# First loads, mask rows and diagonals of a fused block-sparse attention and gated FFN kernel: other queues, other engines, a new order at the head

## The chip, the cores and the metric

The kernel runs on one core of one Trainium2 chip. The metric is the device time of one execution in microseconds (us). The core has five engines with a queue each: TensorE (PE) for matrix products, VectorE (DVE), ScalarE (ACT), GpSimd (POOL), and SyncE (SP), which here only issues DMAs. ScalarE and GpSimd issue DMAs on their own queues too. Each queue is worked off in order, so an instruction that waits holds everything behind it on its engine.

## The reference

The reference has two parts. The first is block-sparse attention over 4 batches, 8 heads, 768 tokens and a head size of 64, in blocks of 32 tokens:

```
scores = q @ k^T / sqrt(64)
mask   = |blk_i - blk_j| <= 1, or blk_i or blk_j is 0 or 23,
         or blk_j is one of sampled_blocks[blk_i] (3 per query block)
attn   = softmax(where(mask, scores, -1e9));  x = attn @ v
```

The second takes the heads side by side (512 wide) through a gated FFN:

```
h    = relu(x @ w_in)                    # 768 x 1024 per batch
conv = 3-tap convolution of h along the tokens, one weight per channel and tap
out  = (h * sigmoid(conv)) @ w_out       # 768 x 512 per batch
```

## The kernel before

All operations are put in a list, and a string, `ORDER`, says in which order they are issued. Each entry is two characters for the operation's number, then a letter for the engine where the operation has a choice (A ScalarE, V VectorE, G GpSimd), then one character for each buffer that it takes. The priorities and costs beside the operations (`{"DVE": 0.45}`) belong to the planner that wrote the string; when the kernel is built, `put_down` only follows the string. An engine's queue is thus the string's order restricted to that engine. Changing the string changes all queues.

The 16 pairs of heads (four to a batch) go through 144 units of eight 128x128 score blocks. For a unit, TensorE computes scores into one of two `st` buffers (`s`, line 773), ScalarE takes the exponential into `pt` (`exp`, line 785, 128x1024), and TensorE multiplies by v (`av`, line 810). VectorE divides by the row sums (`rcp`, `norm`), and `x_tr` or a DMA transpose turns the result into `xT`. Then come the first weight matrix (`f1`, line 914, with `relu` to `hE`), the three taps (`mul`, line 972, and `add`, line 980, on VectorE), tanh on ScalarE (line 1019), `g1` and `g2` on VectorE (lines 1022 and 1027, into `gT`), and the second weight matrix (`f2`, line 844). For one half of the last batch the three taps run on TensorE instead, as products with diagonal matrices (`conv`, line 991). These matrices, `diag`, are made by `dg` (line 391): 8 channel groups by 3 taps, each an identity matrix of 128x128 times one weight per partition, 24 instructions on VectorE.

The mask is part of the score product. Under the 64 rows of k and q in each slot `t` stand 24 rows (partitions 64 to 87): the k side says to which block a key belongs, the q side holds -8000 for a block that the query may not see. The k side comes from `nblk` (line 283) through `m_k` (two copies, for even and odd k columns). The q side comes from the sampled blocks: `ld_sb` (line 254) loads them into `sbi`, `a4` and `a5` (line 296) make `A` and then `mtok`, in two halves, and `m_q0` copies the first half in the order of the tokens into slot 0 (two copies, of 256 and 128 elements). `m_q1` does so for the second half of the queries. `m_h1` repeats the q rows and the k rows for the second head of the pair, `m_r1` repeats `m_q1`'s. The other slots get their mask rows by copies (`m_sq`, `m_sr`) or DMAs on SyncE's queue (`m_dk`, `m_dq`, `m_sp`); `m_back` holds a reordered copy for the later pairs. Copies made by the helper `dcopy` carry line 324 on ScalarE, 326 on GpSimd and 328 on VectorE.

The first pair's q and k arrive in float32 in the output staging tiles `o2s` (`ld_q0`, `ld_k0`: the first half of the queries of each head, and all keys), and are cast to bf16 into `nat` by `cast_q` and `cast_k`. `k_tr` and `q_tr` turn them on TensorE (lines 474 and 514), and `k_cp` and `q_cp` bring them into slot 0. All later pairs come by GpSimd's queue, already cast. Until the first scores, and in gaps after them, TensorE runs 13 wide and 29 narrow dummy products (`warm`, `fill`, line 230).

In the order before, the first DMAs are: on SyncE the first head's k, the sampled blocks, the second head's q, the convolution weights; on ScalarE the first head's q, then the second head's k. The second head's casts are on GpSimd, between its loads. `m_q0` is on ScalarE, and both `m_h1` on VectorE.

Of the kernel before, what the change touches and what calls it, by code (L numbers as in the profile page):

```python
# [25 lines left out]
6z6i6j6v26A36n6o16D06E2h16F45+06w6I16J6x6B6C6G6R06S6H6K56L6M6W16X6T06Y11v1a2iV6p21r6q2jV6N05/V6O6r16/0706U06V6sV6P0
6QV71274175763in1io7907aiq0ir7i17j7b41p1sipV001d2NV4isViL07k51y4/2+2it17n07oiu6Z6+7p0iMiNiOivV1501z513025231531A54
1B5537056iP7s17t7273iw0ix7x07y2v17u1iyA393103211e330347z277787G17H7c2C02wV2xViT12DV47e12EViU7f7L07M7d17l7I37N4iQiF1
7Q17m7RiG7q7r7V07W7v7wiHV22F07AiR2GV2HV7S57X07B2Q17+17/7J0iz080187088892iA7K8c18d8e32RV0iWiViS0iBV32SV7C27O7P7T8h0
8i7U7Y7Z2T0iX2UV7D8m18j48n818302VViC18v0iDiEV8wiI0821iJiYiZ84iKVi/2j0j738o58x08A18B8a8b8f8g8F08G8C18H28k7g18l8p8q  # L30
8K17E08L8y08P08z7hA18M38518Q8D8E8I8R48r1j2i+7FVj18s86V8X18J8Y8Z58N8O8t0900912/V0j8j38Sja8uV8U235Vj9jl1951jm8T192096
8+8/939a09b94jf0jgj497136Vjbj538V1j69c2jc9i1989j9n0999o9d9ejhjn9k43c19p58Vjd9f0je9s19t9u1573a583b23d113g13hV2593i
3j12I03l3k5a3r3u3v02W13n08W2joji9x09yjjA0jpV19g3eV3fV1o9z39C1jr1jsju0jvjtAjwAjP09l09m9D2J19q9K09Ljx09E0jy9P19Q9M2
9R49r9v9wjQ2KV2LVjzVjSjR9A9U09V9B9FjA19H1jT9W59IjBjCAjX19Z19G19N9+jD0jG1jHa50jEjU9/1jZjVjYjFVj+a6jIAa739Oaa19Sabac0
jM12X09Taf0ag9XjN9Yak1alah4k322YVk42ZVk6j/am5jJ0ap0jKa0aqa1a80a9adax1aeaiajay3x3s23w3G3Dk0k5jLVa22jOVjWk1kb3a3k7k2
kckdkear2anaz1aoaC0aDaskp0aH1aIat1aAaE3aJ0k8aBaM0aFaNaGkB1aU1aKkCaLkqaVaO4aZ0aPaQa+kfkgaW5a/2k9kakrkDb219h9J3o3z13A
3m3a43y4au0khkiksb3kEktA2b433pV3BVkFV3avb70kK0b8kLb90kH13CV3qVbc1aX0kIbdaYkJV14kMAbe53H23E03J3I3S3P3Q13T33Vbk0blkQ0
b0kN1bm1b1kRb5kSAl30aR1l4aSl6l5l7kOkPA5lb1ld3tV3b6bp1bqbr4bakT0bu0bbl83L1jkkukG3M3W0aw03K0aT3UbvkW1kUkVV6bz1bw2bAbf
bg1kXbnbokYAbB3bsbH0kZ0bIbtbxk+bM1bybNl01bJ0k/A7lclj2lklml9bR0bCbSl1kj0bO5bh2lebil2V3FV43NVla1lflr3bW1bXbT1bY4kv1bD
kkb/0bK03RA0bE0llbFlslnc0c71c8c13kwbLbPbQbUkxbVbZb+c90lgcc0cdklkyce53XkzA0bGbjkAjqlulhltlvkmc2c31cach1cbciknV2lo3+  # L40
414213/24643lic41lplwlx3OVlqcj2lF1lz0cm0cnlGlAcu1cvcw1co4lBlHly3YV1lIlJV3cz1lClDV0cAcfcB3cE0lO1cFlPlL03ZVc540V1lQV
cG0lMlNAcgcJ1cKm70cO0cPckcllU1cpcqlVm8m9macr0cL5lR0lSmbcscQ2lWAlTAmf1mccx0cW1cycXcCc/0cDl+1l/d0cHcIcMcNcY4d41d5d13
d65mhmgmdmim0VcRcT2mjlX0lYcS1lZAcZd90c+m11dadh1d2dim40d3m2d7mkdb2dj3dm0dnm5d8dr1ds44454c4f4g04k4h4imemn2momlmqcUm3V
m6VmpkolKc61471lE4l048cVctdo1mJ1dcdw0dxdddk0dldt0dy4mv3mxmrmmmwde1mydfmzdB1dCdpmD0dqdJ0dKdumKdD5msdL3mEdO1dvdzdAdE
dF1dPmtmu4d04t4u2mAdT0dUdMmFdNmLdgdQ1dV0dRdY1mBmCmMdZmGe40dSe5mNV1dG2d+4dWdXm/1e91n04eV249V24aVn1V084j4y4q4r1e65
mHA2eaee0d/e0eb2n50efn21n34mmO4sV3dHe10e24z1dI2eg3ej1ekn6e70eo0epn4Vnn0n7V9np4nV3no4oVel1eq04v4H4I34w4x4E4M4J4F24K
4Lne1e8ew1ecexn80n9ey5edeheieB0nfeCemenereG1eHnaAeD2ngAnb0es1ezeL0nceMeAnh1nv1nqet1eI34S4T0eN1eunrndVanwnD2nxnEny
eT1eEeUnk0eFnieJeKeOePeY0nleV4eZnjAbnseQ2eRnGnz4pe3ev4AeS4N04Oe+0eW0f11nmAf2mP1eXmQe/mRf60f0f7mV0f35f4mSnAf82fb1mW
nFnL3nMnHnBntnOnNmTV3nP4GV44BV4nu0nCnIfcfd1fj0mXfkf5mYfl4fo1f9oc1fpft0odmZA0nQfq0oeVnJo90fafufeoao31obAfg0nK4CVo4
o5Afy1fzo60o7nZ1n+oz0nRfv3fA5o8AoAnSfhoBor1otosoC4PV0ouoDov4QVfG0fHff1n/o0fI2fL1fMoi0fmfnfQ0fRo1A1ojfrof1ogfsfN1fw  # L50
fxfV1fWfS4okAohAoEoH2owfX0nT0ol1fBfCfJ0f+0f/g03fKomfOfPnUg61fTg7g85nVoIoxonVoJoyoFoKgb0gcoo1opfUfD1oLfYfZgg1ghg1nW
# [61 lines left out]
def kernel(  # L113
# [74 lines left out]
    op = gr.op  # L188
# [887 lines left out]
```

## Time and profile before

| | |
|---|---|
| median of 3 runs | 207.18 us (206.76 to 207.27) |
| the profiled execution: its time | 207.02 us |
| its span, first to last instruction | 205.2 us |
| granted TensorE clock | 0.998 |
| TensorE busy | 200.1 us, 98% |
| VectorE busy | 184.7 us, 90% |
| ScalarE busy | 189.4 us, 92% (144 exponentials: 140.3 us) |
| GpSimd busy | 60.0 us, 29% |

A row of the timeline has the start, the duration, the engine, the line of the kernel, the operation, what it writes and reads with the shapes, how many instructions are merged into the row, and in brackets the engine's idle time before it and what ended that. SPq, ACTq and POOL rows named DMA are the issuing of a DMA. A row of the groups has the busy time, the mean duration in ns, and the idle time before. TensorE's products overlap in its pipeline, and their ends are modelled, so a busy TensorE need not be at its full rate.

### The profile page before, as it was taken

The page shows a single profiled execution, that of the slowest core. Times are in us where ns is not written, and L with a number is a line of the kernel's source. Part 1 is how long each engine was busy: PE and PEld are TensorE (multiplying, and loading weights), DVE is VectorE, ACT ScalarE, POOL GpSimd, SP SyncE. Part 2 cuts the span into 40 slices and gives each one's busy share as a digit, 9 for nine tenths or more (in the row PEclk, how much of TensorE's full clock was granted, in tenths as well). Part 3 has the DMA queues.
Part 4 walks back from the last instruction along what each step waited for, and adds up shares of the span by engine and source line. Part 5 has one row for each costly group of instructions (what it writes and reads, how often), then busy time and mean ns, then how long its engine had stood idle before and what let it go on. Part 6 is the DMA issues. An engine that isn't in the chain of part 4 may idle for free.

```text
span 205.2 us, 6315 instructions
## 1 busy us (share of the span) xinstructions
PE 200.1 (98%) x2442; PEld 145.2 (71%) x2442; DVE 184.7 (90%) x577; ACT 189.4 (92%) x252; POOL 60.0 (29%) x116
## 2 busy tenths in 40 slices
PE   7999999999999999999999999999999999999994
PEld 5678877877677766766477667766676767787773
DVE  6999999999999998999899979999999737999970
ACT  5899999999999999999799999999999989998843
POOL 5987634326242423114215334710000000000000
PEclk9999999999999999999999999999999999999999
DMA  6999997999989995999969779994040260001305
GB/s 148 191 179 193 188 201 119 143 120 148 144 110 113 124 143 73 244 123 127 222 106 171 116 103 180 133 136 77 0 139 21 78 227 0 3 0 71 139 29 179
DMA packets 50913, 25.45 MB, mean 124 GB/s; under 512 B 35588, under 2 KB 48740, under 8 KB 50884
## 3 DMA queue, kind: packets, MB, share of 16 engines
q0 software_dynamic: 20000, 11.24, 44.5%
q1 hardware_dynamic: 30452, 13.45, 32.8%
q8 instruction: 19, 0.31, 0.6%
q10 hardware_dynamic: 432, 0.36, 0.6%
q14 instruction: 10, 0.08, 0.1%
HBM read 23.09 MB, written 6.29 MB: 143 GB/s over the span
## 4 chain that ended last, share of the span: by engine, by line
PE 78%; ACT 14%; DVE 4%; issue 3%; ACTq 0%
PE st L773 25%; PE mix L914 18%; PE mix L844 15%; PE av L810 13%; ACT pt L785 10%; PE av L230 2%; DVE t L328 2%; ACT hE L934 2%; ACT m L1019 1%; PE st L844 1%; PE mix L740 1%; PE av L991 1%; ACT o2s L324 1%; DVE diag L391 1%; PE mix L536 1%
## 5 line engine op out<-in xcount | busy, mean ns | idle before, releaser
L785 ACT ACTIVATE pt<-st 128x1024 bf16<-128x1024 f32 x144 | 140.3, 1033 | 4.5 <-PE st L773 3.3
L773 PE MATMUL st<-t 88*128 88x256 bf16 (+2 forms) x600 | 93.0, 268 | 0.5 <-ACT pt L785 0.3
L810 PEld LDWEIGHTS <-pt 128*128 128x128 bf16 x1152 | 55.4, 97 | 13.7 <-ACT pt L785 0.4
L773 PEld LDWEIGHTS <-t 88*128 88x128 bf16 x600 | 48.6, 97 | 20.6 <-issue 1.0
L810 PE MATMUL av<-vt,pt 128*128 128x65 bf16 x1152 | 62.4, 193 | 0.1
L914 PE MATMUL mix<-xT,winb 128*128 128x384 bf16 (+2 forms) x288 | 55.7, 308 | 0.1
L972 DVE TENSOR_SCALAR m<-hE,cw 128x382 bf16<-128x382 bf16 (+2 forms) x192 | 49.9, 318 | 3.8 <-ACT hE L934 3.6
L844 PE MATMUL mix<-woutb,gT 128*128 128x512 bf16 (+2 forms) x200 | 49.6, 360 | 0.0
L980 DVE TENSOR_TENSOR m<-m 128x764 bf16<-128x764 bf16 (+2 forms) x64 | 33.4, 531 | 0.2
L914 PEld LDWEIGHTS <-winb 128*128 128x128 bf16 x288 | 24.1, 97 | 8.6 <-issue 0.7
L1019 ACT ACTIVATE m<-m 128x764 bf16<-128x764 bf16 (+2 forms) x32 | 26.2, 826 | 0.0
L844 PEld LDWEIGHTS <-gT 128*128 128x128 bf16 x224 | 18.7, 97 | 8.8 <-DVE gT L1027 0.3
L419 POOL COPY pace<-pt 1x1 bf16<-1x1 bf16 x24 | 7.6, 317 | 50.3 <-ACT pt L785 50.1
L934 ACT ACTIVATE hE<-mix 128x384 bf16<-128x384 f32 (+2 forms) x39 | 18.9, 504 | 0.9 <-PE mix L914 0.4
L721 DVE TENSOR_TENSOR xtok<-av,rcp 128x384 bf16<-128x384 f32 (+2 forms) x36 | 18.2, 507 | 0.3
L1027 DVE TENSOR_TENSOR gT<-m,hE 128x764 bf16<-128x764 bf16 (+3 forms) x36 | 18.0, 508 | 0.3
L239 POOL DMA_DIRECT2D nat<-in_q_dram x23 | 16.9, 736 | 2.0 <-issue 1.6
L936 DVE TENSOR_SCALAR hE<-mix 128x384 bf16<-128x384 f32 x25 | 13.8, 554 | 1.0 <-PE mix L914 0.7
L328 DVE COPY t<-mix 64x384 bf16<-64x384 bf16 (+1 forms) x34 | 13.8, 410 | 0.8 <-PE mix L536 0.2
L1022 DVE TENSOR_SCALAR m<-m 128x764 bf16<-128x764 bf16 (+3 forms) x36 | 12.1, 342 | 0.6 <-ACT m L1019 0.5
L239 POOL DMA_DIRECT2D vn<-in_v_dram x16 | 11.5, 720 | 1.3 <-issue 0.6
L328 DVE COPY t<-stg 64x1536 bf16<-64x1536 bf16 x20 | 11.6, 586 | 0.3
(74 smaller groups left out, 118.9 us busy)
## 6 DMA issues: line engine op xcount, KB each, us to landing
out_dram<-o2s SPq DMA_DIRECT2D x16, 256.0 KB
vn<-in_v_dram POOLq DMA_DIRECT2D x16, 192.0 KB, 5.1
nat<-in_k_dram POOLq DMA_DIRECT2D x15, 192.0 KB, 5.0
out_dram<-o2s SPq DMA_DIRECT2D x15, 128.0 KB
nat<-in_q_dram POOLq DMA_DIRECT2D x6, 192.0 KB, 4.9
winb<-in_moe_w_in_dram POOLq DMA_DIRECT2D x2, 512.0 KB, 7.6
woutb<-in_moe_w_out_dram POOLq DMA_DIRECT2D x4, 256.0 KB, 7.3
nat<-in_q_dram POOLq DMA_DIRECT2D x9, 96.0 KB, 4.9
```

The costliest lines, as they stand in the source:

```text
L239: return op(name, {eng: occ}, lambda e: on(e).dma_start(out=dst(), in_=src), prio, deps, dma=(kind, service), **kw)
L328: nc.vector.tensor_copy(out=dst, in_=src)
L721: nm = op("norm", {"DVE": t_dps(128 * C)}, lambda e: nc.vector.tensor_tensor(out=xtok_t[xk.index][:, 0:C].rearrange("p c h d -> p h c d"), ...
L773: nc.tensor.matmul(out=st[:, 128 * x:128 * (x + n_)], lhsT=t[0:88, 12 + 6 * hh + kc, :], rhs=t[0:88, idx:idx + (n_ - 1) * (2 if P < NPE el ...
L785: nc.scalar.activation(out=pt_t[ptb.index][:, c0:c1], in_=st_t[stb.index][:, c0:c1], func=AF.Exp, bias=0.0, scale=0.125)
L810: nc.tensor.matmul(out=o[:, off:off + 65], lhsT=pt_t[ptb.index][:, 128 * x:128 * x + 128], rhs=V_t[vslot_b[P].index][:, hh, kc, 0:65], sta ...
L844: nc.tensor.matmul(out=acc(), lhsT=gT_t[gb.index][:, ffc, 128 * t:128 * t + 128], rhs=woutb[:, ffc, c0:c1], start=(ffc == 0), stop=(ffc == ...
L914: nc.tensor.matmul(out=mix_t[hb.index][:, w1 * y:w1 * y + w1], lhsT=winb[:, fc, 128 * ffc:128 * ffc + 128], rhs=xT_t[xt_buf[n].index][:, f ...
L934: nc.scalar.activation(out=dst, in_=src, func=AF.Relu, bias=0.0, scale=0.5)
L972: nc.vector.tensor_scalar(out=m_t[cb.index][:, x, y, 0:w], in0=hE_t[heb.index][:, f0 + y, t0 + x:t0 + x + w], scalar1=cw[:, x, f0 + y:f0 + ...
L980: nc.vector.tensor_tensor(out=m[:, a_, :, 0:w], in0=m[:, a_, :, 0:w], in1=m[:, b_, :, 0:w], op=ALU.add)
L1019: th = [op("tanh", {"ACT": t_act(2 * w) + 0.04}, lambda e, cb=cb, w=w: nc.scalar.activation(out=m_t[cb.index][:, 0, :, 0:w], in_=m_t[cb.in ...
```

## The change

The sampled blocks are loaded first of all on ScalarE's queue, followed by the first head's q; SyncE loads the first head's k, then the second head's k and q. In the new string `m_q0` stands on VectorE, right behind `a5`; the `m_h1` of the q rows stands on ScalarE and that of the k rows on VectorE, later. The second k's cast is on ScalarE. `m_dk` reads the k rows of one head twice, so it no longer waits for `m_h1`. The diagonals are GpSimd's, at the very end of its queue, behind its last load. `he_zero`, `ident24`, `m_r1`, `m_sr` and `m_sp` have other places. From the head up to about a third of the kernel, and in its tail, the string has another order; between these the queues of TensorE, VectorE and ScalarE are as before.

```diff
-0J1f0O0I0K1k0L0002103040M05010P1W01X0N060Q1U0070R080S0+A1CA11EA1FG282090/V1DG0a13V15181b290b1g2610c1h0d1i0e1j0f0U0g
...
+0J1f0O0I0K1k0L0002103040M05010P1W01X0N060Q1U0070R281080S0+A1EA21CA1FA29090/V15181b1DG0a1g2610b1h0c1i0d1j0e0U0f0V0g
...
     k0 = first_k(0, "SP", -22, [])
-    q0 = first_q(0, "ACT", -22, [])
-    k1 = first_k(1, "ACT", -21, [q0])
-    ld_sb = op("ld_sb", {"SP": 0.46}, lambda e: nc.sync.dma_start(
+    ld_sb = op("ld_sb", {"ACT": 0.46}, lambda e: nc.scalar.dma_start(
         out=sbi[64:MR], in_=sampled_blocks.bitcast(I32).rearrange("b r -> (b r)").unsqueeze(0).broadcast_to([NB, 6 * NB])),
-        -21, after=[k0], lat=1.8)
-    q1 = first_q(1, "SP", -20, [ld_sb])
+        -22, lat=1.8)
+    q0 = first_q(0, "ACT", -21, [ld_sb])
+    k1 = first_k(1, "SP", -21, [k0])
+    q1 = first_q(1, "SP", -20, [k1])
...
-            mr = [dma("m_dk", "SP", lambda s=s: T_t[s][64:88, 12:24].rearrange("j c s -> j (c s)"),
-                      T_t[0][64:88, 12:24].rearrange("j c s -> j (c s)"), T(4.5 * s - 4), m_k + m_h1[1:], service=0.4)]
+            mr = [dma("m_dk", "SP", lambda s=s: T_t[s][64:88, 12:24].rearrange("j (h c) s -> j h (c s)", h=2),
+                      T_t[0][64:88, 12:18].rearrange("j c s -> j (c s)").unsqueeze(1).broadcast_to([NB, 2, 768]),
+                      T(4.5 * s - 4), m_k, service=0.4)]
...
-                nc.vector.tensor_scalar(out=diag[:, x, f], in0=ident, scalar1=cw[:, x, f:f + 1], scalar2=None,
+                nc.gpsimd.tensor_scalar(out=diag[:, x, f], in0=ident, scalar1=cw[:, x, f:f + 1], scalar2=None,
                                         op0=ALU.mult)
-        o_diag[f] = op("diag", {"DVE": 3 * t_d4(128)}, dg, T(10 + f), [o_cw, o_ident], earliest=14.0)
+        o_diag[f] = op("diag", {"POOL": 1.2}, dg, T(100 + f), [o_cw, o_ident], earliest=130.0)
```

More of the change, by code (lines that the diff above doesn't have):

```diff
@@ L26 @@
[L26 to L50, printed above, removed]
@@ L61 @@
+ig1qaqyAhhQqIhZqX0qKqYqei31qn1qoi4i74i8qfA2qpAii90hR0ihiiia2ibhSA2qz2qAqBqCij1qDikqt1ic0quidAqh0qvAjqih+1qjh/Ail1qk
+qEimAqlA3rl1rmrnArr0rsqP3qJqFqQqLqSqGqRq+rtAqMqTqNrx1ryru1rvro0rwArprH0rIr31rz2rqArAqOrC1rDr90rBqUpiqgqmpcrJ1rE2qZ
+qVrFq/ras70rM0r4rNsd1rGses8qWr0rKr1rO2rbr5rLsfr2rPrQrcr6rdA0r7A2sgrR0rSs9sarTrUrf1sbV3shArVA1rgrer8sirWscrhrirjArk
+rX0rYrZr+s11r/As0s2s3s4s5Vs6
 """
@@ L440, in kq_transposes @@
                        {"ACT": 0.25, "DVE": 0.28, "POOL": 0.45} if x else {"ACT": 0.25, "DVE": 0.28},
-                       alloc=[] if x else [nb], uses=[nb] if x else []) for x in range(2)]
+                       uses=[nb]) for x in range(2)]
             ck = [cast("cast_k", lambda x=x: nat_t[nb.index][:, 1, 384 * x:384 * x + 384], lambda x=x: kf[x][:, 0:384],
-                       -16.6 + 2 * x, [ld_k0[x]], both, uses=[nb])
+                       -16.6 + 2 * x, [ld_k0[x]], both, alloc=[] if x else [nb], uses=[nb] if x else [])
                   for x in range(2)]
```

49 lines of the change are left out of this document (35 added, 14 removed).

## The prediction

> **What bounds the kernel now.** I read the busy shares and the chain that ended last first, then the busy time in stretches, then the timeline of the head on all engines, and last the timeline where GpSimd stops.
>
> ```profile
> span 205.2 us, 6315 instructions
> PE 78%; ACT 14%; DVE 4%; issue 3%; ACTq 0%
> 7.23:10.00 2.77, 2.58 (x29) 1.78 (x27) 2.59 (x9) 2.77 (x4) 2.77 (x5) 1.00 1.15 177
> 140.00:150.00 10.00, 10.00 (x94) 6.42 (x93) 9.94 (x30) 9.94 (x15) 0.00 (x0) 1.00 0.14 35
> ```
>
> The columns of the stretches are length, then busy time and instructions of TensorE, its weight loads, VectorE, ScalarE and GpSimd, granted clock, DMA share and rate. The chain runs 78% over TensorE. In the late stretch TensorE is busy all the time, and VectorE and ScalarE for 9.94 of 10.00 us: work added to VectorE there has next to no room. GpSimd does nothing in it; that is the room that the change uses. So the change can win only in the head, before TensorE is full, and can lose wherever it makes VectorE late.
>
> **The head.** The first scores need the mask rows of the first queries (`m_q0`), the even k rows (`k_cp`) and q (`q_cp`).
>
> ```profile
> 0.74 0.40 SPq L239 DMA_DIRECT2D o2s<-in_k_dram  x1
> 1.18 0.46 ACTq L239 DMA_DIRECT2D o2s<-in_k_dram  x1
> 1.20 0.43 SPq L254 DMA_DIRECT2D sbi<-in_sampled_blocks_dram  x1
> 2.94 0.49 DVE L328 COPY t<-nblk 24x384 bf16<-24x384 bf16 x1
> 2.97 0.69 ACT L324 COPY t<-nblk 24x384 bf16<-24x384 bf16 x1
> 3.69 0.77 ACT L324 CAST nat<-o2s 128x192 bf16<-128x192 f32 x2
> 3.69 0.35 DVE L328 COPY t<-t 24x768 bf16<-24x768 bf16 x1 [0.27 <-ACT t L324]
> 4.16 0.23 DVE L371 MEMSET vt<- 128x12 bf16 x4
> 4.42 0.53 DVE L296 SCALAR_TENSOR_TENSOR A<-sbi,keyid,A 24x24 f32<-24x24 int32 x2
> 4.91 0.50 POOL L326 CAST nat<-o2s 128x384 bf16<-128x384 f32 x1 [1.14 <-DMA o2s<-in_k_dram]
> 4.98 0.84 DVE L296 SCALAR_TENSOR_TENSOR mtok<-sbi,keyid,A 24x384 bf16<-24x384 int32 x1
> 5.04 0.47 ACT L324 COPY t<-mix 64x384 bf16<-64x384 bf16 x1 [0.59 <-PE mix L474]
> 5.85 0.74 DVE L328 COPY t<-mix 64x384 bf16<-64x384 bf16 x2
> 5.86 0.60 ACT L324 COPY t<-mtok 24x128 bf16<-24x128 bf16 x2 [0.34 <-DVE mtok L296]
> 6.53 0.39 PE L773 MATMUL st<-t 88*128 88x384 bf16 x2
> 7.23 7.59 ACT L785 ACTIVATE pt<-st 128x1024 bf16<-128x1024 f32 x8 [0.28 <-PE st L773]
> ```
>
> The first scores start at 6.53, just after ScalarE's mask copies end (5.86 + 0.60 = 6.46), and those waited for `mtok`. Back from there the chain is VectorE's own queue: `a4` starts at 4.42 behind four memsets (4.16), and these behind the copy `m_h1` at 3.69, which waited 0.27 for ScalarE's `m_k`. No wait for the sampled blocks shows at 4.42, so their earlier DMA is not by itself the gain; taking `m_h1` out from ahead of `a4` is.
>
> **VectorE after the change.** `m_k` ends at 2.94 + 0.49 = 3.43; the memsets take it to 3.70, `a4` to 4.25. `a5` has two durations, 0.84 beside GpSimd's cast and 0.61 here:
>
> ```profile
> 8.45 0.17 DVE L286 CAST ident<-ident 24x24 f32<-24x24 bf16 x1
> 8.54 1.86 DVE L328 COPY t<-mix 64x768 bf16<-64x768 bf16 x4
> 11.12 0.61 DVE L296 SCALAR_TENSOR_TENSOR mtok<-sbi,keyid,A 24x384 bf16<-24x384 int32 x1
> 11.76 0.58 DVE L391 TENSOR_SCALAR diag<-ident,cw 128x128 bf16<-128x128 bf16 x3
> 12.37 0.72 DVE L328 COPY t<-mtok 24x384 bf16<-24x384 bf16 x1
> 13.12 0.68 DVE L391 TENSOR_SCALAR diag<-ident,cw 128x128 bf16<-128x128 bf16 x3
> 15.85 0.35 DVE L328 COPY t<-t 24x384 bf16<-24x384 bf16 x1
> 16.12 1.02 ACT L785 ACTIVATE pt<-st 128x1024 bf16<-128x1024 f32 x1 [0.39 <-PE st L773]
> ```
>
> I take 0.61, since the cast of the second k moves to ScalarE: 4.9. VectorE's own price of `m_q0` is not in the trace; the nearest row is `m_q1`, the same reordering copy of 384 elements, 0.72. In two pieces it is 0.6 (ScalarE's) to 0.85; I take 0.80: 5.7. `q_cp` (half of 0.74) ends at 6.1, and the first scores start at about 6.2, 0.33 earlier. With no fill matmul between them the exponential follows at about 6.85 instead of 7.23.
>
> ScalarE must be there by then. From 3.69 it has two casts (0.77), the second k's cast that GpSimd had (0.50 there), two `k_cp` of 0.47 with a transpose between that can make it wait, and `m_h1` (0.35 to 0.69, the rows at 3.69 and 2.97): 6.3 to 6.9. The new wait is `k_cp` behind the second k's cast; if that k lands at 4.9 as before, the exponential moves to 6.9 and no more. Its DMA is issued at the same 1.2, behind the first k on SyncE instead of behind the smaller q on ScalarE, with the same bytes ahead and q after it: I keep the landing at 4 to 4.9. The GpSimd queue, which stood 1.14 us for it, issues its loads some 1.2 us earlier; that ends no wait on this path. SyncE's whole-mask copy (`m_sp`) now waits for `m_r1` ahead of `m_back`, whose readers are pairs loaded far later: cost nothing. `m_dk` now waits for `m_k` alone and is issued some 0.4 earlier: its reader is held by the evictions below, so nothing again.
>
> Further on the gain narrows. `m_h1` (0.35), now after the k copies, and `m_sq` (now after `q_cp` of the second head) put the four evictions of the second pair (1.86, ending at 10.40) at 10.2 to 10.4: gain there 0 to 0.2. Up to the third pair VectorE loses two diagonals (0.58 + 0.68) and takes in `m_r1` (0.35) and `ident24` (0.17): 0.74 less, together 0.75 to 0.95. The exponential at 16.12 is that pair's first; it waited 0.39. ScalarE by itself gives 0.33 to 0.38 there, and 0.39 more if the wait goes whole. I take **0.45** (bounds 0 and 0.77). From there the exponentials and then TensorE carry it on; the other 18 diagonals leave a VectorE that is not what TensorE waited for, so I count nothing for them.
>
> **The diagonals on GpSimd.** There are 24 instructions behind the last load, which GpSimd issues at 133.17. The consumer, the convolution on TensorE, first runs at 192.77, so their own time is hidden. Not hidden is what they do to VectorE:
>
> ```profile
> 1.25 0.29 POOL L263 TENSOR_SCALAR_AFFINE_SELECT ident<-ident 128x128 bf16<-128x128 bf16 x1 [0.28 <-DVE ident L224]
> 35.06 0.54 DVE L972 TENSOR_SCALAR m<-hE,cw 128x382 bf16<-128x382 bf16 x2
> 35.30 0.18 POOL L685 COPY pace<-nat 1x1 bf16<-1x1 bf16 x1
> 71.36 0.55 DVE L980 TENSOR_TENSOR m<-m 128x772 bf16<-128x772 bf16 x1
> 71.39 1.03 POOL L419 COPY pace<-pt 1x1 bf16<-1x1 bf16 x1 [1.20 <-ACT pt L785]
> 79.23 0.82 DVE L328 COPY t<-stg 64x1536 bf16<-64x1536 bf16 x1
> L328 DVE COPY t<-stg 64x1536 bf16<-64x1536 bf16 x4 | 2.2, 549 | 0.1
> 133.17 0.72 POOL L239 DMA_DIRECT2D vn<-in_v_dram  x1 [0.28 <-DVE m L972]
> 158.23 0.53 DVE L1027 TENSOR_TENSOR gT<-m,hE 128x772 bf16<-128x772 bf16 x1
> 159.13 0.38 PE L844 MATMUL mix<-woutb,gT 128*128 128x512 bf16 x1
> 164.58 0.18 DVE L719 RECIPROCAL rcp<-av 128x4 f32<-128x4 f32 x1 [1.20 <-PE av L810]
> 192.77 0.33 PE L991 MATMUL av<-hE,diag 128*128 128x130 bf16 x3
> ```
>
> The two engines get in each other's way. A GpSimd copy of one element takes 0.18 beside multiplications and 1.03 beside additions; a VectorE copy takes 0.82 where a GpSimd DMA is being issued, against a mean of 0.549 (the row without a start, from 140 to 160 us), where GpSimd is idle; `a5` lost 0.23 beside a GpSimd cast of 384 elements. The nearest GpSimd row for a diagonal is the 128x128 select, 0.29 (24 of them are 7.0 us). What VectorE loses for one lies between 0 (the multiplications beside the copy at 35.30 keep their time) and 0.27 (0.82 less 0.549). By the row of `a5`, scaled by elements (128 of 384), it is 0.08; I take 0.055, as some of it falls between VectorE's instructions: 24 x 0.055 = **1.3 us**, bounds 0 and 6.5, within some 15 us from 133.
>
> VectorE's slack is small: the gating product at 158.23 ends 0.37 before the output matmul that reads it (159.13), and VectorE first idles long at 164.58. So TensorE stands for what goes beyond 0.37: 1.3 - 0.37 = **0.9 us**.
>
> The Trainium skill speaks against this part: its page "SBUF — State Buffer", section "Who interferes with whom", says that GpSimd and VectorE share a port pair as an exclusive lock, held for a whole instruction, with the second to issue fully blocked. The rows agree in kind (1.03 against 0.18, 0.82 against 0.549) but not in full, since the copy at 35.30 was not held up by multiplications around it. By the rule taken whole the loss would be 24 x 0.29 = 7.0.
>
> **The rest.** The tail's order is laid anew with the same instructions: 0, give or take 0.3.
>
> **The sum.** The profiled execution took 207.02 (1.8 around its span), 0.16 under the median of the three runs shown. 207.02 - 0.45 + 0.9 = 207.5.
>
> **The rivals.** *GpSimd holds VectorE for longer* (slower). VectorE's loss for one diagonal goes by the share of the GpSimd instruction, as for `a5`: 0.23 of 0.50, so 0.135 of 0.29, and 3.2 us in all; 3.2 - 0.37 - 0.45 gives 209.5. It ends past 207.8 from (0.78 + 0.45 + 0.37) / 24 = 0.067 for one on, close to my 0.055. Held for whole instructions it is 7.0 - 0.37 - 0.45, so 213.2; that is the page's rule, and I give it 0.05 of this rival's 0.33. For it: the back-to-back VectorE. Against: the copy at 35.30.
> *The diagonals fit into VectorE's gaps* (faster): its loss stays under 0.37, so 207.02 - 0.45 = 206.6, or 206.3 if the wait at 16.12 goes whole (0.77); I take 206.4, since the 18 diagonals that VectorE no longer has after 16 us can only help. For it: the same copy. Against: the copy of 0.82. Chance 0.28.
> *The head gives nothing*: the second pair's operands are ready no sooner, and the third's no sooner either because its loads or transposes hold it: 207.02 + 0.9 = 207.9. For it: the evictions that end at 10.40 all the same. Against: the two diagonals that go. Chance 0.09.
>
> **How the numbers follow.** The forecast, near no change, has 0.30. About 0.3%, 0.62 us, is what a measurement of this kernel tells from none, from 206.56 to 207.80 around the median. Faster: 0.20 of the 0.28 of the case in which the diagonals fit; its other 0.08 are inside. Slower: 0.33 of the first rival, 0.05 of the last and 0.04 at the forecast's upper edge, 0.42. Within: 0.26 + 0.08 + 0.04 = 0.38. The range goes from 206.3 to 210.0; the held-whole case and the far end of 0.27 for one are left out. The forecast's own range is 206.9 to 208.2.
>
> **What would show it.** Right: first scores near 6.2, first exponential near 6.85, the wait at 16.12 smaller; GpSimd busy from 133 to about 148; VectorE's stage copies there longer than 0.549 and its multiplications likewise, by some 0.05 for each diagonal, and TensorE idle by under 1 us between 133 and 164. Wrong: VectorE unchanged there (the faster case), or stretches near 0.14 for each diagonal with TensorE waiting on `gT` or `hE` (the slower one), or the first exponential still after 7.1.

## The result, and the profile after

The changed kernel took 209.12 us in the median of 6 runs (208.18 to 210.62) against 207.23 for the kernel before beside it: 1.0105 times, with an interval of 1.0063 to 1.0147. In a second series (told below) it was 208.63, 1.0069 times [1.0049, 1.0089]. It is slower, by some 1.4 to 1.9 us. (A factor and its interval are worked out from all fast runs of a series, so it is not the quotient of the two medians.) The profiled execution was the quickest of the first series: 208.18, with a span of 206.4 where the kernel before had 205.2.

The profile page of the changed kernel, busy time by engine:

```profile
PE 198.9 (96%) x2423; PEld 144.7 (70%) x2442; DVE 183.3 (89%) x554; ACT 190.4 (92%) x252; POOL 81.1 (39%) x139
```

GpSimd has 21 us more than before (60.0), and TensorE is idle for more of the span. Where, the busy time in stretches says; first two rows of the kernel before that the prediction did not show, then the changed kernel (length, then busy time and instructions of TensorE, its weight loads, VectorE, ScalarE and GpSimd, granted clock, DMA share, rate):

```profile
133.00:140.00 7.00, 7.00 (x82) 4.67 (x79) 6.97 (x25) 7.00 (x11) 0.72 (x1) 1.00 1.11 141
150.00:164.00 14.00, 13.98 (x182) 9.97 (x180) 12.87 (x37) 13.69 (x18) 0.00 (x0) 1.00 0.26 74
```
```profile
133.00:140.00 7.00, 6.95 (x77) 4.55 (x77) 6.97 (x22) 7.00 (x11) 6.96 (x9) 1.00 1.15 138
140.00:150.00 10.00, 9.53 (x89) 5.97 (x89) 9.94 (x28) 9.35 (x14) 10.00 (x13) 1.00 0.10 23
150.00:164.00 14.00, 13.26 (x174) 9.38 (x174) 13.87 (x40) 12.98 (x17) 4.84 (x5) 1.00 0.24 74
```

From 133 to 164 GpSimd is busy for 21.80 us in place of 0.72, and TensorE and ScalarE, full or nearly so before, now have idle time. VectorE is no less busy, but gets through fewer instructions: 22 for 25, then 28 for 30. The waits of the changed kernel from 133 to 165 us name who waits for it (engine, line, what is waited for, total, times, longest):

```profile
ACT m L1020 <- DVE m L981: 0.8, 1, 0.8
PE st L774 <- DVE t L328: 0.5, 1, 0.5
PEld L845 <- DVE gT L1028: 0.5, 1, 0.5
PE mix L915 <- DVE hE L937: 0.4, 1, 0.4
```

Among them are `gT` and `hE`, the waits that the prediction named for the slower rival. The groups of VectorE and GpSimd from 133 to 155 us, before and after (count, busy us, mean ns of one, idle before them):

```profile
L972 DVE TENSOR_SCALAR m<-hE,cw 128x386 bf16<-128x386 bf16 x18 | 4.6, 317 | 0.1
L1022 DVE TENSOR_SCALAR m<-m 128x764 bf16<-128x764 bf16 x4 | 1.3, 354 | 0.0
L980 DVE TENSOR_TENSOR m<-m 128x764 bf16<-128x764 bf16 x6 | 3.2, 548 | 0.0
```
```profile
L973 DVE TENSOR_SCALAR m<-hE,cw 128x386 bf16<-128x386 bf16 x16 | 5.0, 374 | 0.1
L1023 DVE TENSOR_SCALAR m<-m 128x764 bf16<-128x764 bf16 x4 | 1.6, 426 | 0.0
L981 DVE TENSOR_TENSOR m<-m 128x764 bf16<-128x764 bf16 x6 | 3.2, 541 | 0.0
L328 DVE COPY t<-stg 64x1536 bf16<-64x1536 bf16 x4 | 2.3, 586 | 0.1
L392 POOL TENSOR_SCALAR diag<-ident,cw 128x128 bf16<-128x128 bf16 x24 | 21.2, 897 | 0.0
```

VectorE's multiplications take 57 and 72 ns longer and its stage copies 586 in place of 549; its additions, with two inputs, mostly keep their time. GpSimd needs 897 ns for a diagonal, three times the 0.29 of the row that it was priced by. What VectorE loses in sum shows in the gating product, which stood at 158.23 before with the output matmul at 159.13:

```profile
159.93 0.52 DVE L1028 TENSOR_TENSOR gT<-m,hE 128x772 bf16<-128x772 bf16 x1
160.50 0.60 PE L845 MATMUL mix<-woutb,gT 128*128 128x512 bf16 x2
```

The product is 1.70 later, the matmul 1.37. The last load, ahead of the diagonals, is issued 0.30 earlier than before (132.87 for 133.17). So VectorE lost 1.70 + 0.30 = 2.0 us in between, **0.083 for each diagonal**, and TensorE 1.37 + 0.30 = **1.67**; the difference, 0.33, is the slack.

The head of the changed kernel (start, duration, engine, line, operation, tiles; count; idle time ahead of the row and what ended it):

```profile
4.35 0.61 DVE L296 SCALAR_TENSOR_TENSOR mtok<-sbi,keyid,A 24x384 bf16<-24x384 int32 x1
4.99 0.50 DVE L328 COPY t<-mtok 24x256 bf16<-24x256 bf16 x2
5.53 0.74 DVE L328 COPY t<-mix 64x384 bf16<-64x384 bf16 x2
5.93 0.98 PE L774 MATMUL st<-t 88*128 88x384 bf16 x7
6.14 0.34 POOL L326 CAST nat<-o2s 128x192 bf16<-128x192 f32 x1 [0.89 <-DMA o2s<-in_q_dram]
6.61 5.82 ACT L786 ACTIVATE pt<-st 128x1024 bf16<-128x1024 f32 x6
12.74 4.91 ACT L786 ACTIVATE pt<-st 128x1024 bf16<-128x1024 f32 x5 [0.31 <-PE st L774]
```

The mask chain went as forecast, a little faster: `m_q0` on VectorE took 0.50 (estimated 0.80). First scores at 5.93 (before 6.53), first exponential at 6.61 (before 7.23). Yet of these 0.62 only 0.30 are left at 133 us. The GpSimd row shows one place: the second q is cast only after a wait of 0.89 for its load, now third on SyncE, and the seventh exponential, at 12.74, is only 0.12 earlier than before, behind a wait of 0.31.

### The profile page after: what moved, and what is told of

It is laid out like the page before. It is cut to its first block, busy times and chain, and to the rows that moved or that the text cites. A ratio compares the mean times of both kernels' runs of the same rounds, so it can differ in the third digit from the quotient of the medians.

```text
span 206.4 us, 6292 instructions
## 1 busy us (share of the span) xinstructions
PE 198.9 (96%) x2423; PEld 144.7 (70%) x2442; DVE 183.3 (89%) x554; ACT 190.4 (92%) x252; POOL 81.1 (39%) x139
## 4 chain that ended last, share of the span: by engine, by line
PE 62%; DVE 16%; ACT 14%; issue 4%; DMA 1%; SPq 1%; ACTq 0%; DVEq 0%
PE st L774 22%; PE mix L915 13%; PE av L811 11%; PE mix L845 11%; ACT pt L786 9%; DVE m L973 4%; DVE t L328 3%; ACT m L1020 2%; DVE m L981 2%; ACT hE L935 2%; DVE gT L1028 1%; DMA stg<-nat 1%; DVE hE L937 1%; PE st L845 1%; DVE m L1023 1%
## 5 line engine op out<-in xcount | busy, mean ns | idle before, releaser
L811 PEld LDWEIGHTS <-pt 128*128 128x128 bf16 x1152 | 56.3, 97 | 14.7 <-issue 0.5
L811 PE MATMUL av<-vt,pt 128*128 128x65 bf16 x1152 | 63.8, 193 | 0.2
L973 DVE TENSOR_SCALAR m<-hE,cw 128x382 bf16<-128x382 bf16 (+2 forms) x192 | 51.8, 327 | 3.7 <-ACT hE L935 3.4
L845 PE MATMUL mix<-woutb,gT 128*128 128x512 bf16 (+2 forms) x181 | 46.3, 358 | 0.7 <-DVE gT L1028 0.2
L915 PEld LDWEIGHTS <-winb 128*128 128x128 bf16 x288 | 23.6, 97 | 8.8 <-issue 1.1
L392 POOL TENSOR_SCALAR diag<-ident,cw 128x128 bf16<-128x128 bf16 x24 | 21.2, 897 | 0.0
```

The source lines that it names most:

```text
L392: nc.gpsimd.tensor_scalar(out=diag[:, x, f], in0=ident, scalar1=cw[:, x, f:f + 1], scalar2=None, op0=ALU.mult)
L811: nc.tensor.matmul(out=o[:, off:off + 65], lhsT=pt_t[ptb.index][:, 128 * x:128 * x + 128], rhs=V_t[vslot_b[P].index][:, hh, kc, 0:65], sta ...
L845: nc.tensor.matmul(out=acc(), lhsT=gT_t[gb.index][:, ffc, 128 * t:128 * t + 128], rhs=woutb[:, ffc, c0:c1], start=(ffc == 0), stop=(ffc == ...
L915: nc.tensor.matmul(out=mix_t[hb.index][:, w1 * y:w1 * y + w1], lhsT=winb[:, fc, 128 * ffc:128 * ffc + 128], rhs=xT_t[xt_buf[n].index][:, f ...
L973: nc.vector.tensor_scalar(out=m_t[cb.index][:, x, y, 0:w], in0=hE_t[heb.index][:, f0 + y, t0 + x:t0 + x + w], scalar1=cw[:, x, f0 + y:f0 + ...
```

## The experiments

Theory A: GpSimd's diagonals slow VectorE at a price for each, 1.7 us on TensorE in all; the head gains 0.3 to 0.5. Rival B: the new order of the head and the tail loses by itself, whatever GpSimd does. Offsets below compare the same exponential in the two profiled executions, that of the kernel before being the one of the prediction; minus is earlier. The diffs leave out the strings and the planner's costs, which change along with the lines shown.

**Run 1 and run 2: each half of the change alone.** Run 1 is the kernel before with its own head and order, with the diagonals alone moved behind GpSimd's last load; run 2 the changed kernel with the diagonals on VectorE in the head:

```diff
 run 1, in the kernel before
-                nc.vector.tensor_scalar(out=diag[:, x, f], in0=ident, scalar1=cw[:, x, f:f + 1], scalar2=None,
+                nc.gpsimd.tensor_scalar(out=diag[:, x, f], in0=ident, scalar1=cw[:, x, f:f + 1], scalar2=None,
 run 2, in the changed kernel
-                nc.gpsimd.tensor_scalar(out=diag[:, x, f], in0=ident, scalar1=cw[:, x, f:f + 1], scalar2=None,
+                nc.vector.tensor_scalar(out=diag[:, x, f], in0=ident, scalar1=cw[:, x, f:f + 1], scalar2=None,
```

> The kernel before with one part of the change alone: the 24 diagonals on GpSimd, behind its last load; head and order are those of before. Theory A (in the changed kernel's trace VectorE falls back by 2.2 us between 133 and 155 us, 0.09 for each diagonal, and TensorE by 1.7, because the two engines wait for each other): VectorE falls back by about 2.2 here too, and the time is 208.3 to 209.2; a little of the loss may come back where the diagonals left VectorE in the head. Rival B (the new order of the head and the tail loses the time, and the stretch at 133 us is hidden): 206.8 to 207.3.

> The changed kernel with one part undone: the diagonals back on VectorE, behind the same neighbours as before (the first two groups behind cw). Theory A: the loss at 133 us is gone and the head's gain of 0.3 stays, less what the two groups cost the head: 206.7 to 207.1. Rival B: slower than before as the changed kernel is, 208.2 to 209.2.

Run 1: 208.34 against 206.96, 1.0069 times [1.0044, 1.0095]. Run 2: 208.03, 1.0050 times [1.0032, 1.0068]. Run 1's stretches from 133 us:

```profile
140.00:150.00 10.00, 9.53 (x88) 5.99 (x88) 9.94 (x27) 9.35 (x14) 10.00 (x13) 1.00 0.10 28
150.00:164.00 14.00, 13.26 (x174) 9.44 (x175) 13.83 (x40) 12.87 (x17) 4.58 (x5) 1.00 0.23 67
```

TensorE's busy times are those of the changed kernel to the hundredth, with the old head and the old order in front. The exponentials stood 0.57 earlier until 140 us and 1.13 later from 162 us on: 1.70 lost. So theory A holds for this half, and rival B cannot be all of it. But run 2, outside the ranges of both, refutes theory A's other half: the new head and order, with the diagonals back in VectorE's queue, are slower by 0.5%, not faster. Part of that belongs to the diagonals: in run 2's trace nine of them run on VectorE between 21.91 and 24.4 us, the product behind them that TensorE waits 0.45 for (`xtok`) starts at 26.32 (25.81 in run 3, which has no diagonals there), and the 22nd exponential loses 0.54.

**Run 3 and run 4: the diagonals late.** Both keep the new head and order. In run 3 the diagonals go on VectorE into its late idle time (6 at 163.6, 18 at 167.1 us); in run 4 GpSimd does them, held back by a copy of one element of the 129th exponential's output (from 164.2 us on):

```diff
 run 4, in the changed kernel
+    held = all_pt[128]
+    op("hold", {"POOL": 0.12}, lambda e: nc.gpsimd.tensor_copy(out=pace_t, in_=pt_t[held.index][0:1, 0:1]), T(130), uses=[held])
```

> The changed kernel, its diagonals on VectorE in idle time that the trace shows there late: two groups of three behind the gating product that ends at 163.4 (idle 1.2), six behind the copy that ends at 166.9 (idle 3.4); 24 x 0.19 = 4.6 us of work in 4.6 us of idle time. Theory A: the head's gain whole and no loss at 133, 206.5 to 206.9, the shortest of these four with the next one. Rival B: 208.2 to 209.2. If the gaps are too tight, VectorE's multiplications behind them start up to 0.5 late, and the time is up to 0.5 longer.

> The changed kernel, its diagonals still on GpSimd, but held back by a copy of one element of the exponential of unit 128 (about 163 us), so that they run where VectorE is mostly idle. Theory A: a diagonal takes 0.3 instead of the 0.6 to 1.9 seen at 133 to 155, 24 of them end at about 171, VectorE loses under 0.5, and the time is 206.5 to 207.0. Rival B: 208.2 to 209.2. A third theory, that GpSimd's work slows the core wherever it is put (by power or the write of the tiles), says 208.2 or more as well, with the loss at 163 to 171 instead of 133 to 155.

Run 3: 207.37, 1.0004 times [0.9979, 1.0028]. Run 4: 207.51, 1.0024 times [1.0010, 1.0038]. Run 3 loses nothing from 133 to 164 us (offset +0.35 at 133, +0.31 at 162). So the place, beside a full VectorE, is what makes the diagonals dear. Run 4 shows it once more at its end. Undisturbed, its diagonals take 0.59 each and not the 0.3 expected, so only half of them are done when VectorE resumes its multiplications, first in run 4, then in run 3:

```profile
170.93 2.13 DVE L973 TENSOR_SCALAR m<-hE,cw 128x382 bf16<-128x382 bf16 x6 [3.43 <-ACT hE L935]
170.65 1.62 DVE L972 TENSOR_SCALAR m<-hE,cw 128x382 bf16<-128x382 bf16 x6 [0.50 <-ACT hE L934]
```

The last twelve diagonals run beside VectorE up to 179.3 us, and from 162 us to the last exponential run 4 goes from +0.59 to +1.03, run 3 from +0.31 to +0.14: about 0.6 lost, 0.05 for each of the twelve. That is again theory A; but neither run shows its head gain of 0.3, and both lie above the times that it gave them (206.5 to 206.9 and 206.5 to 207.0). Their heads, run 4's rows first for TensorE, then run 3's for ScalarE, say why:

```profile
4.37 0.50 PE L474 MATMUL mix<-ident,nat 128*128 128x128 bf16 x3
6.09 0.74 PE L229 MATMUL av<-warm 128*128 128x128 bf16 x5
6.62 1.30 PE L774 MATMUL st<-t 88*128 88x384 bf16 x8
```
```profile
6.33 0.47 ACT L323 COPY t<-av 64x384 bf16<-64x384 bf16 x1 [0.95 <-PE av L474]
7.36 5.74 ACT L785 ACTIVATE pt<-st 128x1024 bf16<-128x1024 f32 x6
```

In the profile of the changed kernel the same rows were shorter:

```profile
4.37 0.34 PE L475 MATMUL mix<-ident,nat 128*128 128x128 bf16 x3
5.38 0.44 PE L230 MATMUL av<-warm 128*128 128x128 bf16 x5
```

Same start, 4.37, same instructions: three transposes take 0.34 there and 0.50 here. Single 128-column matmuls follow each other at 0.055 us there and at 0.107 here (their spacing). In run 3 ScalarE's second k copy therefore waits 0.95 for TensorE, and the first exponential stands at 7.36 instead of 6.61. The moment at which the spacing goes from 0.107 to 0.055 differs between executions, though TensorE starts at 1.15 to 1.17 in all of them. All profiled executions but that of run 10, with this moment, the first exponential and the 109th, at 133.39 us, as offsets to the kernel before:

| kernel | head | short spacing from, us | first exponential | at 133 us |
|---|---|---|---|---|
| before | old | 6.2 | 7.23 | 133.39 |
| before again (run 12) | old | 4.7 | +0.01 | -0.30 |
| run 1 | old | 5.2 | -0.17 | -0.57 |
| run 5 | old | 6.1 | -0.03 | +0.14 |
| run 6 | old, mask short | 5.7 | -0.11 | -0.17 |
| changed again (run 11) | new | 3.9 | -0.63 | +0.10 |
| changed | new | 4.4 | -0.61 | -0.30 |
| run 2 | new | 4.6 | -0.53 | +1.09 |
| run 8 | new | 6.2 | +0.14 | +0.40 |
| run 9 | new | 6.2 | +0.15 | +0.30 |
| run 3 | new | 6.4 | +0.13 | +0.35 |
| run 7 | new | 7.0 | +0.22 | +0.64 |
| run 4 | new | 7.3 | +0.30 | +0.62 |

The moment can only be read where narrow matmuls follow each other, so it is uncertain by up to 0.6 (run 5: still long at 5.46, short at 6.10).

With the old head the first exponential hardly cares: it hangs on the mask. The new head takes the mask out of the way, and then TensorE's transposes and fill matmuls are the path: 0.5 to 0.6 earlier if the short spacing is there by 4.6, 0.1 to 0.3 later if it comes after 6. And the first exponential does not settle the rest: the new heads lose 0.6 to 0.9 more by the ninth exponential (run 2 1.2; run 3 is at +0.80 there, the changed kernel at +0.08), and win back some 0.5 at the tenth, of which 0.38 is a wait of the execution that they are compared with (run 12 below). The steps fall at the fifth (up to 0.63), the seventh (0.35 to 0.48) and the ninth exponential (0.17).

**Run 5 and run 6: the old head, improved.** Run 5 is the kernel before with the diagonals moved as in run 3, to late gaps of VectorE. Run 6 adds the short mask chain, with the loads and TensorE's order left as before:

```diff
 run 6, in the kernel before
-            mr = [dma("m_dk", "SP", lambda s=s: T_t[s][64:88, 12:24].rearrange("j c s -> j (c s)"),
-                      T_t[0][64:88, 12:24].rearrange("j c s -> j (c s)"), T(4.5 * s - 4), m_k + m_h1[1:], service=0.4)]
+            mr = [dma("m_dk", "SP", lambda s=s: T_t[s][64:88, 12:24].rearrange("j (h c) s -> j h (c s)", h=2),
+                      T_t[0][64:88, 12:18].rearrange("j c s -> j (c s)").unsqueeze(1).broadcast_to([NB, 2, 768]),
+                      T(4.5 * s - 4), m_k, service=0.4)]
```

> The head, the order and all queues of the kernel before; only the 24 diagonals move, still on VectorE, into its late idle time (two groups from about 163 us, six from about 167). Theory A (sharing costs, room in VectorE's queue gains): without the two diagonals in the head the wait at 16.12 goes and the exponentials run 0.5 to 0.6 earlier from the tenth on, as in the run with only the diagonals moved; GpSimd does nothing at 133 to 155, so nothing is given back: 206.3 to 206.6, median about 206.4, faster than both kernels. Rival B (the late place costs as much, since VectorE's idle time there covers the tail's other work): same gain up to 160 us, but given back after it: 207.0. Rival C (the gain seen at the tenth exponential was the luck of one execution): 207.0 with the offset from the tenth on under 0.2.

> The run before this one with the head's short chain added: the copy of the second half mask goes behind the k copies on ScalarE's side, the mask rows of the first queries go to VectorE right behind the mask, the mask rows for later slots read the first half twice; TensorE's order with its fill matmuls, the loads and their queues stay as before. Theory A with the clock (the head gains only if TensorE's clock has risen by the time that the first scores' operands stand): clock up by about 6.3: first exponential at 6.8 to 7.0 and 206.0 to 206.2; clock up later: first exponential at 7.2 to 7.5 and 206.4 to 206.7. Rival D (the head loses by its new load order, not by the clock): here the load order is the old one, so first exponential at 6.9 and 206.1 whatever the clock does. Rival E (the moved copies are late for the second pair): first exponential early, but the fifth to ninth 0.3 to 0.6 late, 206.8.

Run 5: 207.05 against 206.95, 1.0000 times [0.9985, 1.0016]. Run 6: 206.92, 0.9996 times [0.9980, 1.0012]. Neither beats the kernel before. In run 5's profile the tenth exponential is 0.44 earlier, as theory A says. But in run 12, the kernel before itself, it is 0.37 earlier too, so the step does not come from the moved diagonals (rival C). Later places eat it; one of them is a load that lands late:

```profile
90.50 0.55 DVE L327 COPY t<-stg 64x1536 bf16<-64x1536 bf16 x1 [0.63 <-DMA stg<-nat]
```

That is one execution; the median over 12 runs is what counts, and it is no gain. The late place itself costs nothing here (against rival B): from 133 us to the end the offset stays at +0.13 to +0.14. Run 6, ScalarE:

```profile
7.12 1.94 ACT L785 ACTIVATE pt<-st 128x1024 bf16<-128x1024 f32 x2 [0.31 <-PE st L773]
9.57 7.68 ACT L785 ACTIVATE pt<-st 128x1024 bf16<-128x1024 f32 x8 [0.52 <-PE st L773]
```

The first exponential, at 7.12, misses theory A's 6.8 to 7.0 for a short spacing by 6.3 (it came at 5.7). The third waits 0.52 and is 0.51 late, and the fifth to ninth with it: rival E. It loses no more than that, 0.11 at the tenth.

**Run 7 and run 9: fills and copies instead of diagonals.** Both are run 3 with 24 instructions more on GpSimd, at the place where the changed kernel has its diagonals, that serve nothing: fills with zero of a 128x128 tile, then copies of the identity into it.

```diff
 run 7, in run 3
+    blank = sb.tile([128, 128], BF16, tag="blank", name="blank")
+    for x in range(8):
+        op("blank", {"POOL": 1.2}, lambda e: [nc.gpsimd.memset(blank, 0.0) for _ in range(3)], T(100))
 run 9, in run 7
-        op("blank", {"POOL": 1.2}, lambda e: [nc.gpsimd.memset(blank, 0.0) for _ in range(3)], T(100))
+        op("blank", {"POOL": 1.2}, lambda e: [nc.gpsimd.tensor_copy(out=blank, in_=ident) for _ in range(3)], T(100))
```

> The run with the diagonals in VectorE's gaps (207.4, TensorE offsets +0.3 up to 136 us), and in addition 24 fills with zero of one 128x128 tile on GpSimd, where the changed kernel has the diagonals: writes, no reads. They serve nothing. Theory A (each access of GpSimd takes a turn of a shared port): the fills stretch what VectorE does by about half of 0.09, 24 x 0.045 = 1.1 us on VectorE and 0.6 behind its slack on TensorE: 208.0; fills beside the two-input additions are stretched too. Rival F (only GpSimd's reads collide, its writes not): VectorE keeps its times, 207.4. Rival G (a GpSimd instruction holds VectorE for its whole time): by 0.1 to 0.2 each, 2.4 to 4.8 on VectorE, 209.3 or more.

> As the run with 24 fills on GpSimd beside the diagonals in VectorE's gaps, but each fill is a copy of the 128x128 identity: a read and a write of one tile where the fill only writes and the diagonal reads, multiplies and writes. The copies serve nothing. The 24 fills moved no exponential by more than 0.1. Theory A2 (what collides are GpSimd's reads of SBUF): the copies stretch VectorE's multiplications and its single-input copies by 0.08 to 0.11 per pair as the diagonals did and are held up beside two-input additions; 24 x 0.05 to 0.09 = 1.2 to 2.2 us on VectorE, 0.7 to 1.7 on TensorE: 207.8 to 208.8. Rival (it is the length of the diagonal's multiplication, 0.59 alone, not the read): copies as short as the fills (0.20 to 0.25) and TensorE loses under 0.3: 207.1 to 207.4.

Run 7: 207.06 against 206.95, 0.9998 times [0.9983, 1.0012]. Run 9: 208.67 against 207.26, 1.0070 times [1.0048, 1.0093]. The same six multiplications of VectorE near 137 us, alone (run 3), beside fills (run 7), beside copies (run 9) and beside diagonals (changed kernel), each with GpSimd's row:

```profile
136.98 1.46 DVE L972 TENSOR_SCALAR m<-hE,cw 128x382 bf16<-128x382 bf16 x6
```
```profile
137.39 1.66 DVE L972 TENSOR_SCALAR m<-hE,cw 128x382 bf16<-128x382 bf16 x6
134.52 6.54 POOL L1046 MEMSET blank<- 128x128 bf16 x24
```
```profile
137.53 2.13 DVE L972 TENSOR_SCALAR m<-hE,cw 128x382 bf16<-128x382 bf16 x6
134.18 10.54 POOL L1046 COPY blank<-ident 128x128 bf16<-128x128 bf16 x24
```
```profile
136.57 1.80 DVE L973 TENSOR_SCALAR m<-hE,cw 128x382 bf16<-128x382 bf16 x6
133.62 21.22 POOL L392 TENSOR_SCALAR diag<-ident,cw 128x128 bf16<-128x128 bf16 x24
```

With about six copies beside them, one to each, the multiplications take 0.67 longer, 0.11 for a copy; with about three diagonals 0.34, again 0.11 for one. Fills cost 0.03 each here, and TensorE 0.1 in all. The 24 copies cost TensorE 1.65 (exponentials +0.30 at 133, +1.95 at 162), what 24 diagonals cost, though they are done in half the time. So it is not GpSimd's time that VectorE pays for but what GpSimd reads: theory A2. The price is not one of the multiplications alone: VectorE's additions, in run 3 and beside the copies of run 9, where the copies that run beside them take 0.50 to 0.67 in place of 0.30:

```profile
L980 DVE TENSOR_TENSOR m<-m 128x764 bf16<-128x764 bf16 x6 | 3.2, 546 | 0.0
L980 DVE TENSOR_TENSOR m<-m 128x764 bf16<-128x764 bf16 x6 | 3.5, 590 | 0.0
```

The expectation for run 9 (207.8 to 208.8) holds, that for run 7 (208.0) misses on the low side: theory A's half price for a write was too high, and rival F, that writes do not collide, came nearly true.

**Run 8: every diagonal twice.**

```diff
-            for x in range(3):
+            for x in (0, 1, 2, 0, 1, 2):
```

> The changed kernel with every diagonal computed twice on GpSimd, 48 instructions instead of 24 (same result). Theory A (a price of about 0.09 for each that runs beside a full VectorE): GpSimd needed 21 us for 24 of them, so some 10 to 12 more fall before VectorE's first long idle time at 164 and cost 0.9 to 1.1 more, the rest are hidden: 0.9 to 1.1 above the changed kernel, 209.2 to 210.2. Rival H (the loss is one stall around two of the instructions at about 146 to 150 us, not a price for each): no more than the changed kernel, 208.2 to 209.1. Rival G (held whole): 24 more times 0.29, 215.

209.48 against 206.95, 1.0110 times [1.0088, 1.0132]. GpSimd's row from 134 us, and the last seven diagonals, from 168.2 us, where VectorE is mostly idle:

```profile
134.32 37.64 POOL L392 TENSOR_SCALAR diag<-ident,cw 128x128 bf16<-128x128 bf16 x48
L392 POOL TENSOR_SCALAR diag<-ident,cw 128x128 bf16<-128x128 bf16 x7 | 4.1, 593 | 0.0
```

The exponentials go from +0.40 at 133 to +2.77 at 162 us: 2.4 lost in place of 1.7. There are some 14 diagonals more ahead of 165 us, before VectorE first idles long, and 0.7 more on TensorE, 0.05 for each; theory A had put it at 0.9 to 1.1. One stall at one place (rival H) would not have grown. An undisturbed diagonal takes 593 ns.

**Run 10: TensorE nearly idle in the head.** Run 3 with the warm-up and fill matmuls cut to 8 columns:

```diff
-        def warm_mm(e, n=256 if x < NWARM else 128):
+        def warm_mm(e, n=8):
```

> The run with the new head and the diagonals in VectorE's gaps, with every warm-up and fill matmul cut from 256 or 128 columns to 8: same instructions in the same order, but TensorE is nearly idle up to the first transposes. Theory C (TensorE's narrow matmuls go to the short spacing only after a stretch of work, and the new head's gain hangs on that moment): the short spacing comes after 8 us instead of 4.4 to 7.0, the first exponential at 7.5 or later, the scores of the first units at double spacing hold ScalarE up, 0.5 to 1.5 over that run's 207.4: 207.9 to 208.9. Rival (the moment does not hang on TensorE's own work): short spacing between 4.4 and 7.0 as in the other runs and 207.4 or a little less, since the fills no longer stand ahead of the transposes.

210.91 against 207.26, 1.0181 times [1.0153, 1.0209], some 3.5 us over run 3.

```profile
5.89 1.86 PE L773 MATMUL st<-t 88*128 88x384 bf16 x8
6.94 1.94 ACT L785 ACTIVATE pt<-st 128x1024 bf16<-128x1024 f32 x2
9.91 1.02 ACT L785 ACTIVATE pt<-st 128x1024 bf16<-128x1024 f32 x1 [1.03 <-PE st L773]
```

The short spacing comes only between 19.4 and 20.0 us, so it hangs on TensorE's own work: theory C. Its two numbers missed. The loss is more than twice the most that was expected (1.5), since six of the first nine exponentials, up to 18.9 us, wait for scores at double spacing. And the first exponential is early, 6.94, although the spacing is long: the fills that stand ahead of the first scores are gone. With long spacing it thus seems to be the transposes and the fills together that make the new head late; that is read from this one profile.

**Run 11 and run 12: both kernels once more**, for second profiles.

> The changed kernel once more, for a second profiled execution and a median on the same chip as the other runs of this call. Theory (the head's gain hangs on when the narrow matmuls go to the short spacing, 4.4 us in the first profile; the loss at 133 to 155 does not): short spacing at 5 to 7 us, first exponential 0.1 earlier to 0.3 later than in the kernel before, and from 116 to 124 us the same loss of 1.6 to 1.8 on TensorE: 208.7 to 209.2 in that execution, median 209.0. Rival (the head always gains 0.3 and more, the first median was high by chance): first exponential at 6.6 again and a median of 208.2.

> The kernel before once more, for a second profiled execution. If its times of 206.5 to 206.8 and of 207.2 to 207.5 come from the head and from single late transfers too, the exponentials differ by 0.2 to 0.6 from those of the first profile in steps at a few places (first scores, tenth exponential, 22 us, 98 us) and are parallel in between; if the wait of 0.39 ahead of the tenth exponential belongs to the kernel, it is there again.

Run 11: 208.63 against 207.26, 1.0069 times [1.0049, 1.0089]. It missed part of its expectation: the short spacing came at 3.9, and the first exponential at 6.60; but its median of 208.63 is not the rival's 208.2, nor theory's 209.0. VectorE's and TensorE's loss is there again (exponentials +0.10 at 133, +1.94 at 162: 1.84).

Run 12, a single execution, took 206.79. The copy of v in the first profile of the kernel before, then run 12's rows for it and for those from 12.37 to 16.12 in the prediction:

```profile
10.32 0.55 DVE L328 COPY vt<-vn 128x768 bf16<-128x768 bf16 x1
```
```profile
10.34 0.34 DVE L328 COPY vt<-vn 128x768 bf16<-128x768 bf16 x1
12.19 0.53 DVE L328 COPY t<-mtok 24x384 bf16<-24x384 bf16 x1
12.75 0.58 DVE L391 TENSOR_SCALAR diag<-ident,cw 128x128 bf16<-128x128 bf16 x3
7.24 11.37 ACT L785 ACTIVATE pt<-st 128x1024 bf16<-128x1024 f32 x12 [0.25 <-PE st L773]
```

The diagonals are in the same place in VectorE's queue, yet the copy of v takes 0.34 (0.55 in the first profile), `m_q1` 0.53 (0.72), the second diagonals 0.58 (0.68), and twelve exponentials run without a gap: the wait of 0.39 ahead of the tenth is not there. So the wait does not belong to the kernel: it is in one of its two profiles and not in the other.

## Why the prediction was right or wrong

The range, 206.3 to 210.0, holds the result; the forecast itself, 207.5 and no measurable change, does not, since the kernel is slower by well over 0.3%. Slower had the largest chance, 0.42. That the range holds is owed to its width of 3.7 us: both terms of the sum were off, and in the same direction. With measured terms its own sum closes on the profiled execution: 207.02 - 0.30 (head, as left at 133 us) + 1.67 (TensorE behind the diagonals) - 0.17 (tail) = 208.22 against 208.18. The median of that series lies 0.9 above this execution, which the sum does not explain. The signs came out mixed: multiplications and stage copies longer, as forecast, but TensorE idle by 1.26 us from 133 to 164 (0.02 before), not by under 1, and waiting on `gT` and `hE`.

- **The price of a diagonal** is the step that failed. The row of `a5`, scaled by elements, gave 0.08; measured is 0.083 here and 0.084 in run 1 (2.02 in all). That it came so near is partly luck: the measured price is a mean over 0.11 beside multiplications and little beside additions, and no run tries the scaling by elements. The discount to 0.055, for what falls between VectorE's instructions, was wrong: VectorE, busy for 9.94 of 10.00 us, had next to no such gaps. The slack of 0.37 was right (0.33). That makes 0.9 into 1.67. The threshold that the text gave itself, 0.067, was passed.
- **GpSimd's own time**, 0.29 by the 128x128 select, is 0.59 undisturbed and 0.90 here; it is busy to 155, not 148. This does not change the loss, as the copies show.
- **The first rival** had the direction and the waits (`gT`, `hE`) right but not the price: 0.135 by the share of GpSimd's time (and its sum gives 209.4, not 209.5). Taken whole, the Trainium skill's rule ("SBUF — State Buffer", section "Who interferes with whom"), which that section states for VectorE instructions in its 2-port modes, gave 7.0 us against 2.0 measured. In run 9 a copy of 0.30 cost a multiplication 0.11. The same section states that a VectorE instruction with two inputs in SBUF contends with a GpSimd instruction that reads, not with one that only writes. For the multiplications, with one such input, the runs show the like: 0.11 beside copies, 0.03 beside fills. For the additions beside diagonals it is mostly GpSimd that is slowed (897 ns in the mean for 593 undisturbed, about 1.09 us beside an addition and up to 1.94 beside two gating products) and VectorE hardly (541 after, 548 before); beside the copies of run 9 both are (590 for 546).
- **The second rival**, diagonals that fit into gaps, fell: its witness, multiplications that kept their time beside a copy of one element, does not carry over to a whole tile, whose copy costs a multiplication 0.11 (run 9). Room there is, but only from 163 us on, and not for all of GpSimd's 24 (runs 3 and 4).
- **The head** was right in its mechanism and mostly not a gain. The mask chain came out as laid down, with `m_q0` at 0.50. But of the 0.45, up to 0.39 was the wait at 16.12, which is not there in run 12; taking the two diagonals out gains nothing in the median (run 5). The -0.30 that is left at 133 us is no gain either: run 12, the kernel before itself, stands at -0.30 too, and against it the other profiles of the new head in the table are 0.40 to 1.39 later there. And the earlier first scores hang on TensorE's spacing, which the prediction did not price: even its lower bound, a gain of 0, was too high for executions with the short spacing after 6 us. Run 3 has the whole new head at 1.0004 times [0.9979, 1.0028]. So the third rival, the head gives nothing, came true in the median.
- **The tail** moved by -0.17 (offset +1.39 at 162 us, +1.22 at the last exponential), inside its 0.3; five other profiles with the new tail show the same -0.17.

What stays open: why the two series of the changed kernel differ by 0.5, and what of the new order costs 0.6 to 0.9 up to the ninth exponential. The late second q (0.89 in front of its cast) was seen, but not tried alone. Run 2 is slower than run 3 by 0.7, and at 133 us its profile is 0.74 behind: 0.54 of it falls at the 22nd exponential, behind the diagonals (above), and 0.21 at the 28th, for which the cause stays open.

## What to carry to other kernels

Work given to an idle engine is not free because its consumer is far away, if it slows a full engine beside it: price it by what it reads, and put it where the full engine idles for as long as the work takes. A wait in one profiled execution that hangs on collisions or on a landing is no gain until a second execution shows it again. When a change takes one chain off the start of a kernel, price the next chain with the longest spacing of matmuls that any execution shows.

## What the runs showed of the hardware

- VectorE's multiplications pay about 0.11 us for a 128x128 GpSimd instruction that reads SBUF beside them, whether that takes 0.30 (copy) or 0.61 (diagonal, beside multiplications), and 0.03 for one that only writes (runs 7 and 9, changed kernel).
- TensorE's 128-column matmuls went from a spacing of 0.107 to 0.055 us at 3.9 to 7.3 us, in executions that all began its work at 1.15 to 1.17, and at 19.4 to 20.0 when that work was thin. The Trainium skill ("TensorE: Matmul & The Clock Gate", Part 1, "What's actually happening") tells of a free-running window of some 3.4 us. The spread of 3.4 us agrees with that; a moment within half a microsecond, as its section "What you observe" has it, does not. The granted clock shows nothing of this (1.00 from 7 to 19 us in run 10, at the long spacing); the spacing of single instructions does.
